# Decode attention in fp32: the vector engines' share of the value rows goes from 64 to 72 of 128, the row maxima are turned onto every partition, and two pieces of work change places

## The chip, the cores and the metric

The kernel runs on one core of a Trainium2 chip. The metric is device time in microseconds of one execution, as the median of several. The core has engines that run side by side, each through its own list of instructions in order: TensorE (PE, with its weight loads PEld), VectorE (DVE), ScalarE (ACT) and GpSimd (POOL). SyncE (SP) starts the large transfers from the chip's main memory (HBM), which 16 DMA engines carry out in the order in which SP issued them. Matrix products land in a small second memory, PSUM, here in tiles of 512 columns called `acc`, `bank` and `bank2`; GpSimd does not work on PSUM here.

## What is computed

One decode step of two transformer layers with shared weights and a shared cache: attention, a gated MLP, and both once more.

```python
q = (x @ wq).reshape(B, Sq, H, Dh)            # B = 2, Sq = 1, H = 32, Dh = 128
scores = einsum("bhqd,bhkd->bhqk", q, k_cache) * Dh ** -0.5     # Sk = 8192 keys a head
p = softmax(scores)
o = einsum("bhqk,bhkd->bhqd", p, v_cache)
x = x + o @ wo                                # then x = x + MLP(layernorm(x)); all of it twice
```

Everything is fp32. Keys and values of one layer are 2 x 268 MB, and each of the two layers reads nearly all of them, so that the core reads 1152.39 MB in one execution.

## The kernel before, in words

**Items.** A batch and two neighbouring heads form an item (the last two heads are items of their own, "singles"). Partition p holds `rows` = 128 keys of its head, 64 partitions for each of the two heads, so that the keys of an item are a tile of 128 partitions x 128 rows x 128 numbers, 64 KB a partition and 8192 KB in all; the values the same. One DMA brings the keys of an item, one its values. The arena (`space` in the traces) has room for three such tiles, and SP loads in the order K(n), V(n-1), K(n+1), V(n) and so on: each load takes the place of the third load ahead of it, and is issued once all readers of that one are done. Sixteen rows are a "part" (JC = 16), and a place is freed part by part. Layer 0 goes through the items upwards, layer 1 downwards.

**Scores.** The query of an item is spread over the partitions by a small matrix product (`query`, L687) into one of two stretches of `bank`. DVE multiplies the keys by it in three units of 48, 48 and 32 rows (`multiply`, L769). POOL adds the upper 64 numbers of each row to the lower 64 (L798). DVE sums what is left (`add_up`, L801), which is the score. The sum of the third unit of an item is made in the turn of the next item, ahead of its first product.

**Softmax.** `peak` takes the maximum of each partition's scores (L825) and turns the column of 128 maxima into a row, by a product of the column with the unit matrix (L827, into `turned`, a part of `bank2`). `highest` takes the maximum of each head from the row (L833, on one partition) and spreads it over the partitions by a second product (L835). `softmax` has ACT make the exponentials `prz` from it (L850, L858).

**Values.** TensorE multiplies the first 64 rows of each partition by their weights (`values`, L944, 16 products of four rows, each run in two passes). The other 64 rows (FOLD = 4 parts) are *folded* by DVE and POOL for all items but the first and last few of a layer (`folds`; 49 foldings in all). `weigh(n, True)` copies the weights of these rows into a stretch of `bank2` called `share` (L905) and has DVE multiply the first 32 rows by them (L912); POOL then adds halves onto each other, 32 rows to 16, to 8, to 4 (L915). `weigh(n, False)` does the same with the last 32 rows, one item later, and adds the two results of four rows (L917). `folded` adds the four rows into the accumulator by one product (L922), and frees the values' place.

**Order.** Each engine's order is the order in which `attention` writes it out, unit by unit; nothing reorders it. In the turn of item n, p is the item before it and f the one before p. Ahead of the first unit stand the last `add_up` and `peak` of p and `weigh(f, False)`. Behind the first unit (j == 0) stand the `query` of the next item and `folded(f)`; `highest` and `softmax` of p come at j == 0 too where p has three units. At j == 1 come the sums and `values(p)`, and every second item `gather` (L967, L968, DVE), which reads the finished accumulator; the items in between have a reciprocal there (`inverse`, L877). At j == 2 comes `weigh(p, True)`.

Accesses to the same PSUM tile by two engines are kept apart by waits: a product that writes `bank` or `bank2` holds up the DVE instruction behind it that uses the same tile.

Of the kernel before, what the change touches and what calls it, by code (L numbers as in the profile page):

```python
# [9 lines left out]
F32 = mybir.dt.float32  # L10
AF = mybir.ActivationFunctionType
ALU = mybir.AluOpType
AX = mybir.AxisListType
PSUM = bass.MemoryType.PSUM

P = 128
# [3 lines left out]
DH = 128  # L20
# [4 lines left out]
JC = 16  # L25
# [18 lines left out]
END = RING + NPLACE * PLACE  # L44
HELD = 5
SPLIT = (18, 18, 12, 16)
FOLD = 4


class Item:  # L50
# [75 lines left out]
def decode_layers(ctx, tc, x_in, kc, vc, wq, wo, wg, wu, wd, out):  # L126
# [32 lines left out]
    def part_at(at, n):  # L159
        return space[:, at:at + n]  # L160
# [180 lines left out]
    def name(kind, layer, n):  # L341

        return kind, 1 if n in (KEYS_HELD if kind == "k" else VALUES_HELD) else layer, n
# [170 lines left out]
    turned = bank2[:, 4 * GH:4 * GH + P]  # L514
    pair, four = bank2[:, 4 * GH + P:4 * GH + P + 2], bank2[:, 4 * GH + P + 2:4 * GH + P + 6]
    low = bank2[:, 4 * GH + P + 6:]
    share = low[:, :FOLD * JC]
    kept = psum1.tile([P, JC, DH], F32, name="kept")

    mid = bank[:, CW + 2 * DH:]  # L520
# [16 lines left out]
    def small(p, n):  # L537

        if n > 2:
            return turned[0:p, 0:n]  # L540
        return pair[0:p, 0:n]
# [70 lines left out]
    def attention(layer):  # L612
# [208 lines left out]
                ready.pop(key)  # L821

        def peak(n):
            m = work.tile([P, 1], F32, name="m")
            nc.vector.reduce_max(m, S[n][:, :ITEMS[n].rows], axis=AX.X)  # L825
            mT[n] = small(1, P)
            nc.tensor.transpose(mT[n], m, ident)  # L827

        def highest(n):

            heads = ITEMS[n].heads
            m1 = work.tile([1, 2], F32, name="m1")
            nc.vector.reduce_max(m1[:, :heads], mT.pop(n).rearrange("p (i q) -> p i q", i=heads), axis=AX.X)  # L833
            mT[n] = small(P, 2)
            nc.tensor.matmul(mT[n][:, :heads], ones[0:1, :], m1[:, :heads], start=True, stop=True)  # L835

        def weights_of(n):

            if ITEMS[n].heads == 2:
                return prz.rearrange("p a e -> p (a e)")  # L840
            return prz[:, n - PAIRS, :]
# [44 lines left out]
        def accumulator(n):  # L886
            return acc[:, (n // B + 1) % 2 if n < PAIRS else (n - PAIRS) // B, :]

        def completes(i):

            return i > 0 and ITEMS[seq[i - 1]].h == ITEMS[seq[i]].h

        def folds(n):

            return (2, 1)[layer] < n < PAIRS - 3

        def weigh(n, first):

            lo = ITEMS[n].parts - FOLD
            if first:  # L900
                of_halves = weights_of(n)[:, 8 + 4 * JC * lo:8 + 4 * JC * (lo + FOLD)]
                of_halves = of_halves.rearrange("p (g a e) -> p a g e", a=4, e=4)
                for i in range(2):
                    at = slice(i * HALF, i * HALF + HALF)
                    nc.scalar.copy(share[at].rearrange("p (g e) -> p g e", e=4), of_halves[at, i])  # L905
            rows = FOLD // 2 * JC
            begin = 0 if first else rows
            at = arena.live[name("v", layer, n), lo][0]
            t = part_at(at, FOLD * PART).rearrange("p (j d) -> p j d", d=DH)
            of_rows = share[:, begin:begin + rows].unsqueeze(2).to_broadcast([P, rows, DH])  # L910
            u = t[:, begin:begin + rows]
            nc.vector.tensor_tensor(out=u, in0=u, in1=of_rows, op=ALU.mult)  # L912
            while rows > 4:
                rows //= 2
                nc.gpsimd.tensor_tensor(out=u[:, :rows], in0=u[:, :rows], in1=u[:, rows:2 * rows], op=ALU.add)  # L915
            if not first:
                nc.gpsimd.tensor_tensor(out=t[:, :4], in0=t[:, :4], in1=u[:, :4], op=ALU.add)  # L917

        def folded(n):

            key, lo = name("v", layer, n), ITEMS[n].parts - FOLD
            nc.tensor.matmul(  # L922
                accumulator(n)[0:16, :], owner[:, 8 * ITEMS[n].b:8 * ITEMS[n].b + 16],
                part_at(arena.live[key, lo][0], 4 * DH), start=False, stop=completes(seq.index(n)),
            )
            for k in range(lo, lo + FOLD):
                done((key, k))
            ready.pop(key)

        def values(i, lo=0, hi=8):  # L930

            n = seq[i]
            it, key, pr = ITEMS[n], name("v", layer, n), weights_of(n)
            t = ready[key]
            left = not (layer == 0 and n in VALUES_HELD)
            gs, less = it.rows // 4, folds(n)
            if less:
                gs -= 4 * FOLD
            begins = not completes(i)
            for g in range(4 * lo, min(gs, 4 * hi)):  # L940
                c = g % 4
                m = 8 * it.heads
                at = m * g + m // 2 * (1 - it.b)
                nc.tensor.matmul(  # L944
                    accumulator(n)[32 * c:32 * c + m, :], pr[:, at:at + m],
                    t[g // 4][:, g % 4 * 4:g % 4 * 4 + 4, :].rearrange("p j d -> p (j d)"),
                    start=(begins and g < 4), stop=(completes(i) and g >= gs - 4 + less),
                )
                if left and g % 4 == 3:
                    done((key, g // 4))  # L950
            if left and 4 * hi >= gs and not less:
                ready.pop(key)
# [103 lines left out]
        for i, n in enumerate(seq):  # L1056
            last = i == N - 1
            p = seq[i - 1] if i else None

            v = {N - 2: None, N - 1: N - 3}.get(i, i - 1) if layer == 0 else i - 1  # L1060
            f = seq[i - 2] if i > 1 and folds(seq[i - 2]) else None
            a = seq[i - 2] if i > 1 and completes(i - 2) and not (layer == 0 and last) else None

            soon = layer == 1 and i in (1, 4)
            first = layer == 1 and i == 1
            us = units(n)

            ahead = p is not None and several(p)
            if first:
                query(seq[i + 1])  # L1070
            if first or ahead:
                add_up(p, *units(p)[-1])
                peak(p)
            if f is not None:
                weigh(f, False)
            if first:
                highest(p)
                softmax(p)
            for j, (k, m) in enumerate(us):
                multiply(n, k, m)  # L1080
                if j == 0 and not last and not first and (i or layer == 0):
                    query(seq[i + 1])
                if j == 0 and f is not None:
                    folded(f)
                if at_once(n, k) and k == 0:
                    add_up(n, k, m)
                if j == 1 and first:
                    values(v)
                    total(p)
                if j == 0 and p is not None and not first and not ahead:  # L1090
                    add_up(p, *units(p)[-1])
                    peak(p)
                if j == (0 if soon or ahead else 1) and p is not None and not first:
                    highest(p)
                    softmax(p)
                if j == (1 if several(n) else 2) and not first:
                    if p is not None:
                        total(p)
                        inverse(p)
                    if a is not None:  # L1100
                        gather(a)
                        if p < PAIRS:
                            context(a)
                    if v is not None and v >= 0:
                        values(v)
                    if a is not None and p >= PAIRS:
                        context(a)
                late_sum = len(us) == 3 and j > 0
                if late_sum and j == 2:
                    add_up(n, *us[0])  # L1110
                if j == 2 and i and folds(p):
                    weigh(p, True)
                if j > late_sum and (n, us[j - 1][0]) in prod:
                    add_up(n, *us[j - 1])
                if j == 3 and first:
                    inverse(p)
                if j == (2 if several(n) else 3) and a is not None and p < PAIRS:
                    divide(a, several(n))
                if j == 1 and late is not None:
                    divide(late)  # L1120
            late = a if a is not None and p >= PAIRS else None
            if layer == 1 and i == 0:

                nc.vector.scalar_tensor_tensor(qsb, acc[:, 0, :], rstd, qsb, op0=ALU.mult, op1=ALU.add)
# [3 lines left out]
        if layer == 0:  # L1128
            values(N - 2)
        peak(n)  # L1130
        highest(n)
        softmax(n)
        if layer == 0:
# [182 lines left out]
```

## Time and profile before

| | |
|---|---|
| median of three runs | 2679.16 us (2679.13 to 2679.84) |
| the profiled execution | 2680.14 us, of which the span from first to last instruction 2678.3 us |
| busy DVE, POOL, PE, ACT | 2194.3, 2015.2, 817.5, 186.2 us |
| read from HBM | 1152.39 MB, 430 GB/s over the span |

Times in the profile are from the start of the span. In rows of the timeline the first number is the start, the second the duration (of several instructions, from the first start to the last end), both in us; in brackets stands how long the engine had been idle before, and what ended that. In rows of groups, "x98 | 432.7, 4415 | 27.3" means 98 instructions, 432.7 us busy, 4415 ns each, 27.3 us of idle time ahead of them.

### The profile page before, as it was taken

The numbers are of one execution on the slowest core, as the hardware profiler recorded it, in microseconds if no ns is written. First come the engines' busy times: TensorE is split into PE (matmuls) and PEld (weight loads), VectorE is DVE, ScalarE is ACT, GpSimd is POOL, SyncE is SP. The second block draws the span as 40 slices with busy tenths as digits, with TensorE's granted clock in tenths as the row PEclk, the third lists the DMA queues.
The fourth block names the chain that finished last, engine by engine and source line by source line (L and its number), as shares of the span: only waits on it lengthen the run. The fifth ranks groups of instructions, "written<-read, shape, count | busy, mean of one in ns | idle before, by whom it ended". The sixth has DMA issues, their size and how long they took to land.

```text
span 2678.3 us, 13402 instructions
## 1 busy us (share of the span) xinstructions
PE 817.5 (31%) x5030; PEld 256.9 (10%) x5030; DVE 2194.3 (82%) x919; ACT 186.2 (7%) x890; POOL 2015.2 (75%) x608
## 2 busy tenths in 40 slices
PE   1312222232223222334663322222222222222266
PEld 0100000000000000011221000000000000000022
DVE  4869999999999999967038789999999999998940
ACT  0000000000000000001026000000000000000000
POOL 2548999998999989944028469899999988998930
PEclk8665555655555555566986655555565555655568
DMA  9999999999999999999999999999999999999999
GB/s 423 436 430 433 437 434 431 434 435 431 432 436 433 431 435 433 433 429 427 420 416 430 436 432 432 434 430 437 432 430 437 434 431 434 434 433 433 432 431 388
DMA packets 29336, 1153.26 MB, mean 431 GB/s; under 512 B 3384, under 2 KB 3416, under 8 KB 4184
## 3 DMA queue, kind: packets, MB, share of 16 engines
q1 hardware_dynamic: 29088, 1152.40, 99.8%
q8 instruction: 39, 0.64, 0.1%
q14 instruction: 25, 0.20, 0.0%
q10 hardware_dynamic: 184, 0.02, 0.0%
HBM read 1152.39 MB, written 0.01 MB: 430 GB/s over the span
## 4 chain that ended last, share of the span: by engine, by line
DMA 43%; DVE 38%; POOL 10%; PE 7%; issue 2%; ACT 1%; ACTq 0%; SPq 0%; POOLq 0%; DVEq 0%
DMA space<-in_A_k_cache_dram 33%; DVE space L769 19%; DVE scores L801 9%; DVE space L912 7%; POOL space L915 7%; DMA space<-in_A_v_cache_dram 4%; DMA space<-in_B_w_down_dram 2%; PE acc L944 2%; PE acc L922 2%; POOL space L798 1%; POOL space L917 1%; DMA space<-in_B_w_up_dram 1%; DMA space<-in_A_wo_dram 1%; PE bank L687 1%; PE acc L1026 1%
## 5 line engine op out<-in xcount | busy, mean ns | idle before, releaser
L798 POOL TENSOR_TENSOR space<-space 128x3072 f32<-128x3072 f32 (+4 forms) x221 | 1124.9, 5110 | 234.6 <-DVE space L769 196.1
L769 DVE TENSOR_TENSOR space<-space,bank 128x6144 f32<-128x6144 f32 (+4 forms) x223 | 1111.0, 4984 | 220.5 <-DMA space<-in_A_k_cache_dram 144.5
L915 POOL TENSOR_TENSOR space<-space 128x2048 f32<-128x2048 f32 (+2 forms) x294 | 796.9, 2710 | 163.5 <-DVE space L912 146.6
L801 DVE TENSOR_REDUCE scores<-space 128x48 f32<-128x3072 f32 (+4 forms) x223 | 563.9, 2550 | 17.5 <-POOL space L798 17.3
L944 PE MATMUL acc<-space,prz 128*16 128x512 f32 (+1 forms) x2528 | 430.0, 846 | 380.3 <-DMA space<-in_A_v_cache_dram 372.2
L912 DVE TENSOR_TENSOR space<-space,bank 128x4096 f32<-128x4096 f32 x98 | 432.7, 4415 | 27.3 <-PE bank L827 27.3
L827 PE MATMUL bank<-ident,m 128*1 128x128 f32 x68 | 24.4, 358 | 420.7 <-DVE m L825 420.6
L944 PEld LDWEIGHTS acc<-space,prz 128*16 128x16 f32 (+1 forms) x2528 | 87.1, 124 | 663.4 <-issue 464.4
L850 ACT ACTIVATE nbs<-bank 128x2 f32<-128x2 f32 (+1 forms) x68 | 11.6, 171 | 1937.9 <-PE bank L835 1904.5
L687 PE MATMUL bank<-qsb,home 36*128 36x128 f32 x60 | 23.4, 492 | 367.8 <-DVE space L769 351.1
L585 POOL TENSOR_TENSOR rstd<-ve,few 128x1 f32<-128x1 f32 x4 | 2.2, 561 | 174.4 <-DVE ve L583 174.4
L687 PE MATMUL bank<-qsb,wide 36*128 36x128 f32 x60 | 23.2, 486 | 348.3 <-DVE space L769 333.2
L922 PE MATMUL acc<-space,few 128*16 128x512 f32 x98 | 92.5, 1047 | 63.3 <-POOL space L917 63.3
L1227 DVE STREAM_TRANSPOSE gu<-acc 128x288 f32<-128x288 f32 x4 | 1.9, 482 | 85.5 <-ACT acc L1225 85.5
L917 POOL TENSOR_TENSOR space<-space 128x512 f32<-128x512 f32 x49 | 62.1, 1268 | 3.8
L858 ACT ACTIVATE prz<-scores,nbs 64x128 f32<-64x128 f32 (+1 forms) x128 | 50.7, 396 | 12.3 <-POOL prz L848 8.8
L827 PEld LDWEIGHTS bank<-ident,m 128*1 128x1 f32 x68 | 5.4, 79 | 477.6 <-issue 433.9
L687 PEld LDWEIGHTS bank<-qsb,home 36*128 36x128 f32 x60 | 14.7, 304 | 378.2 <-DVE space L769 360.3
L791 ACT ACTIVATE space<-space 128x128 f32<-128x128 f32 x164 | 48.4, 296 | 19.7 <-DVE space L769 16.6
L687 PEld LDWEIGHTS bank<-qsb,wide 36*128 36x128 f32 x60 | 14.5, 300 | 358.0 <-DVE space L769 341.6
L967 DVE TENSOR_TENSOR acc<-acc,few 128x512 f32<-128x512 f32 x34 | 23.5, 691 | 25.0 <-PE acc L944 25.0
L835 PE MATMUL bank<-m,few 1*128 1x2 f32 (+1 forms) x136 | 39.0, 354 | 15.1 <-DVE m L833 15.1
(120 smaller groups left out, 584.5 us busy)
## 6 DMA issues: line engine op xcount, KB each, us to landing
space<-in_A_v_cache_dram SPq DMA_DIRECT2D x7, 4096.0 KB
space<-in_A_k_cache_dram SPq DMA_DIRECT2D x6, 4096.0 KB
space<-in_B_w_gate_dram SPq DMA_DIRECT2D x9, 1152.0 KB
space<-in_B_w_up_dram SPq DMA_DIRECT2D x9, 1152.0 KB
space<-in_B_w_down_dram SPq DMA_DIRECT2D x8, 1152.0 KB
space<-in_A_wq_dram SPq DMA_DIRECT2D x9, 1024.0 KB
space<-in_A_wo_dram SPq DMA_DIRECT2D x2, 4608.0 KB
space<-in_A_k_cache_dram SPq DMA_DIRECT2D x4, 2048.0 KB
```

Source lines behind the costliest of these rows:

```text
L687: nc.tensor.matmul(qb[n], of_row, qsb[rows, m * DH:(m + 1) * DH], start=True, stop=True)
L769: nc.vector.tensor_tensor(out=u[:, :r, :], in0=t[:, :r, :], in1=qb[n].unsqueeze(1).to_broadcast([P, r, DH]), op=ALU.mult)
L791: nc.scalar.activation(u[:, j, :], u[:, j, :], AF.Copy, accum_out=S[n][:, base(n, k) + j:base(n, k) + j + 1])
L798: nc.gpsimd.tensor_tensor(out=half, in0=half, in1=u[:, :r, DH // 2:], op=ALU.add)
L801: nc.vector.tensor_reduce(out=S[n][:, base(n, k):base(n, k) + own_rows(n, k, m)], in_=prod.pop((n, k)), axis=AX.X, op=ALU.add)
L835: nc.tensor.matmul(mT[n][:, :heads], ones[0:1, :], m1[:, :heads], start=True, stop=True)
L858: nc.scalar.activation(pr[at, lo:].rearrange("p (g e) -> p g e", e=4)[:, 0:it.rows // 2 * it.heads:2 * it.heads, :], s[at, :it.rows].rearr ...
L912: nc.vector.tensor_tensor(out=u, in0=u, in1=of_rows, op=ALU.mult)
L915: nc.gpsimd.tensor_tensor(out=u[:, :rows], in0=u[:, :rows], in1=u[:, rows:2 * rows], op=ALU.add)
L917: nc.gpsimd.tensor_tensor(out=t[:, :4], in0=t[:, :4], in1=u[:, :4], op=ALU.add)
L922: nc.tensor.matmul(accumulator(n)[0:16, :], owner[:, 8 * ITEMS[n].b:8 * ITEMS[n].b + 16], part_at(arena.live[key, lo][0], 4 * DH), start=F ...
L944: nc.tensor.matmul(accumulator(n)[32 * c:32 * c + m, :], pr[:, at:at + m], t[g // 4][:, g % 4 * 4:g % 4 * 4 + 4, :].rearrange("p j d -> p ...
```

## The change

Five edits in one:

- FOLD counts rows now, and is 72: the first weighing takes 32 rows (EARLY), the second 40. POOL reduces 40 rows by adding the last 8 onto the first 8, and then as before from 32. TensorE multiplies 56 rows, in 14 products instead of 16.
- The column of maxima is given to TensorE 128 times over (`to_broadcast`), so that the product leaves the whole row of maxima on every partition of `turned`. `highest` takes the maxima of the two heads on all partitions and hands them to `softmax` from SBUF; the second product, L835, is gone.
- This product is a function of its own, `turn`, and is written behind `weigh(f, False)`; in `peak` it stood ahead of it.
- The query of the next item is written behind the third product of an item of three units; it stood behind the first.
- The fourth part of the values (rows 48 to 63) is read by both now, rows 48 to 55 by TensorE and the rest by the fold, and is freed by the fold.

```diff
-FOLD = 4
+FOLD = 72
+EARLY = 32
...
         def peak(n):
-            m = work.tile([P, 1], F32, name="m")
-            nc.vector.reduce_max(m, S[n][:, :ITEMS[n].rows], axis=AX.X)
-            mT[n] = small(1, P)
-            nc.tensor.transpose(mT[n], m, ident)
+            mT[n] = work.tile([P, 1], F32, name="m")
+            nc.vector.reduce_max(mT[n], S[n][:, :ITEMS[n].rows], axis=AX.X)
+
+        def turn(n):
+
+            m, mT[n] = mT[n], turned
+            nc.tensor.transpose(turned, m.to_broadcast([P, P]), ident)
 
         def highest(n):
 
             heads = ITEMS[n].heads
-            m1 = work.tile([1, 2], F32, name="m1")
-            nc.vector.reduce_max(m1[:, :heads], mT.pop(n).rearrange("p (i q) -> p i q", i=heads), axis=AX.X)
-            mT[n] = small(P, 2)
-            nc.tensor.matmul(mT[n][:, :heads], ones[0:1, :], m1[:, :heads], start=True, stop=True)
+            m1 = work.tile([P, 2], F32, name="m1")
+            nc.vector.reduce_max(m1[:, :heads], mT[n].rearrange("p (i q) -> p i q", i=heads), axis=AX.X)
+            mT[n] = m1
...
+        def folded_rows(n):
+
+            lo = ITEMS[n].rows - FOLD
+            at = arena.live[name("v", layer, n), lo // JC][0]
...
+            return lo, part_at(at + lo % JC * DH, FOLD * DH)
+
         def weigh(n, first):
...
-            rows = FOLD // 2 * JC
-            begin = 0 if first else rows
...
+            begin, end = (0, EARLY) if first else (EARLY, FOLD)
+            rows = end - begin
...
             nc.vector.tensor_tensor(out=u, in0=u, in1=of_rows, op=ALU.mult)
             while rows > 4:
-                rows //= 2
-                nc.gpsimd.tensor_tensor(out=u[:, :rows], in0=u[:, :rows], in1=u[:, rows:2 * rows], op=ALU.add)
+                less = 1 << (rows - 1).bit_length() - 1
+                nc.gpsimd.tensor_tensor(
+                    out=u[:, :rows - less], in0=u[:, :rows - less], in1=u[:, less:rows], op=ALU.add
+                )
+                rows = less
...
             if less:
-                gs -= 4 * FOLD
+                gs -= FOLD // 4
...
             if f is not None:
                 weigh(f, False)
+            if first or ahead:
+                turn(p)
...
-                if j == 0 and not last and not first and (i or layer == 0):
+                if j == (2 if len(us) == 3 else 0) and not last and not first and (i or layer == 0):
                     query(seq[i + 1])
```

Two engines' lists show what moves, each in the turn of one item in the middle of layer 0 (`bank_125` is `bank2`; "waits" names the engines or DMA queues whose semaphores an instruction waits for; lines of the changed kernel are 1 to 17 higher). TensorE, from the last value products of one item to the first of the next, before:

```order
L944 MATMUL acc<-space,prz 16x512 x15
L827 MATMUL bank_125<-ident,m 1x128 [waits DVE_49,Activation_49]
L687 MATMUL bank<-qsb,wide 128x128 [waits DVE_49]
L922 MATMUL acc<-space,few 16x512 [waits Pool_49]
L835 MATMUL bank_125<-m_763,few 128x2 [waits DVE_49]
L944 MATMUL acc<-space,prz 16x512 [waits DMAHW0_49,DVE_49,Activation_49]
```

and with the change:

```order
L957 MATMUL acc<-space,prz 16x512 x13
L688 MATMUL bank<-qsb,home 128x128 [waits DVE_49]
L831 MATMUL bank_125<-ident,m 128x128 [waits DVE_49,Activation_49]
L935 MATMUL acc<-space,few 16x512 [waits Pool_49]
L957 MATMUL acc<-space,prz 16x512 [waits DMAHW0_49,DVE_49,Activation_49]
```

The query has moved ahead of the turning of the maxima and stands right behind the value products; the product of the folded rows no longer has the spreading of the maxima behind it.

DVE in the same stretch, from the last sum of the item before to its third product, before:

```order
L801 TENSOR_REDUCE scores<-space 128x32 [waits Pool_49]
L825 TENSOR_REDUCE m<-scores 128x1 [waits DVE_49]
L912 TENSOR_TENSOR space<-space,bank_125 128x4096 [waits PE_49]
L769 TENSOR_TENSOR space<-space,bank 128x6144 [waits DMAHW1_49]
L833 TENSOR_REDUCE m_593<-bank_125 1x2
L769 TENSOR_TENSOR space<-space,bank 128x6144 [waits PE_49]
L877 RECIPROCAL rinv<-bank_125 128x4 [waits PE_49]
L769 TENSOR_TENSOR space<-space,bank 128x4096
```

and with the change:

```order
L802 TENSOR_REDUCE scores<-space 128x32 [waits Pool_49]
L826 TENSOR_REDUCE m<-scores 128x1 [waits DVE_49]
L921 TENSOR_TENSOR space<-space,bank_125 128x5120
L770 TENSOR_TENSOR space<-space,bank 128x6144 [waits DMAHW1_49,PE_49]
L837 TENSOR_REDUCE m_581<-bank_125 128x2 [waits PE_49]
L770 TENSOR_TENSOR space<-space,bank 128x6144
L880 RECIPROCAL rinv<-bank_125 128x4 [waits PE_49]
L770 TENSOR_TENSOR space<-space,bank 128x4096
```

The second weighing (40 rows, 5120 numbers) and the second product lose their waits for TensorE; the first product and the maxima of the heads have one instead. POOL's list gains one addition of 128x1024 in each second weighing, and SP issues the same transfers in the same order.

More of the change, by code (lines that the diff above doesn't have):

```diff
@@ L516, in decode_layers @@
     low = bank2[:, 4 * GH + P + 6:]
-    share = low[:, :FOLD * JC]
+    share = low[:, :FOLD]
     kept = psum1.tile([P, JC, DH], F32, name="kept")
@@ L895, in folds @@
             return (2, 1)[layer] < n < PAIRS - 3
+        def folded_rows(n):
+            lo = ITEMS[n].rows - FOLD
+            at = arena.live[name("v", layer, n), lo // JC][0]
+            assert all(arena.live[name("v", layer, n), k][0] == at + (k - lo // JC) * PART for k in range(lo // JC, 8))
+            return lo, part_at(at + lo % JC * DH, FOLD * DH)
         def weigh(n, first):
-            lo = ITEMS[n].parts - FOLD
+            lo, t = folded_rows(n)
             if first:
-                of_halves = weights_of(n)[:, 8 + 4 * JC * lo:8 + 4 * JC * (lo + FOLD)]
+                of_halves = weights_of(n)[:, 8 + 4 * lo:8 + 4 * (lo + FOLD)]
                 of_halves = of_halves.rearrange("p (g a e) -> p a g e", a=4, e=4)
@@ L905, in weigh @@
                     nc.scalar.copy(share[at].rearrange("p (g e) -> p g e", e=4), of_halves[at, i])
-            rows = FOLD // 2 * JC
-            begin = 0 if first else rows
[L908 to L911, printed above, removed]
+            begin, end = (0, EARLY) if first else (EARLY, FOLD)
+            rows = end - begin
+            t = t.rearrange("p (j d) -> p j d", d=DH)
+            u = t[:, begin:end]
+            of_rows = share[:, begin:end].unsqueeze(2).to_broadcast([P, rows, DH])
             nc.vector.tensor_tensor(out=u, in0=u, in1=of_rows, op=ALU.mult)
             while rows > 4:
-                rows //= 2
-                nc.gpsimd.tensor_tensor(out=u[:, :rows], in0=u[:, :rows], in1=u[:, rows:2 * rows], op=ALU.add)
+                less = 1 << (rows - 1).bit_length() - 1
[3 more added lines that the diff above has]
+                rows = less
             if not first:
@@ L919, in folded @@
         def folded(n):
-            key, lo = name("v", layer, n), ITEMS[n].parts - FOLD
+            key = name("v", layer, n)
+            lo, t = folded_rows(n)
             nc.tensor.matmul(
-                accumulator(n)[0:16, :], owner[:, 8 * ITEMS[n].b:8 * ITEMS[n].b + 16],
-                part_at(arena.live[key, lo][0], 4 * DH), start=False, stop=completes(seq.index(n)),
+                accumulator(n)[0:16, :], owner[:, 8 * ITEMS[n].b:8 * ITEMS[n].b + 16], t[:, :4 * DH],
+                start=False, stop=completes(seq.index(n)),
             )
-            for k in range(lo, lo + FOLD):
+            for k in range(lo // JC, ITEMS[n].parts):
                 done((key, k))
@@ L946, in values @@
                     t[g // 4][:, g % 4 * 4:g % 4 * 4 + 4, :].rearrange("p j d -> p (j d)"),
-                    start=(begins and g < 4), stop=(completes(i) and g >= gs - 4 + less),
+                    start=(begins and g < 4), stop=(completes(i) and g >= gs - 4 and not (less and c == 0)),
                 )
@@ L1092, in attention @@
                     peak(p)
+                    turn(p)
                 if j == (0 if soon or ahead else 1) and p is not None and not first:
@@ L1130, in attention @@
         peak(n)
+        turn(n)
         highest(n)
```

## The prediction

> **What bounds the kernel now.** I read the page first: busy times, the rows of the DMA and the chain that ended last.
>
> ```profile
> PE 817.5 (31%) x5030; PEld 256.9 (10%) x5030; DVE 2194.3 (82%) x919; ACT 186.2 (7%) x890; POOL 2015.2 (75%) x608
> DMA  9999999999999999999999999999999999999999
> GB/s 423 436 430 433 437 434 431 434 435 431 432 436 433 431 435 433 433 429 427 420 416 430 436 432 432 434 430 437 432 430 437 434 431 434 434 433 433 432 431 388
> q1 hardware_dynamic: 29088, 1152.40, 99.8%
> DMA 43%; DVE 38%; POOL 10%; PE 7%; issue 2%; ACT 1%; ACTq 0%; SPq 0%; POOLq 0%; DVEq 0%
> ```
>
> No slice of the span has the DMA engines below nine tenths, while DVE stands at 82%. The chain gives DVE 38% all the same, so I looked at whether the transfers ever wait for the engines. First the rate by stage: items without folding at the start of layer 0, then the folded items of layers 0 and 1.
>
> ```profile
> 45.00:200.00 155.00, 34.85 (x218) 11.89 (x218) 125.62 (x40) 5.04 (x22) 82.77 (x14) 0.60 1.00 433
> 240.00:1080.00 840.00, 211.12 (x915) 60.95 (x908) 782.26 (x251) 45.47 (x195) 764.86 (x219) 0.57 1.00 433
> 1640.00:2500.00 860.00, 218.39 (x929) 63.53 (x929) 801.17 (x259) 47.05 (x202) 783.21 (x223) 0.57 1.00 433
> ```
>
> Behind the stage come busy us of PE, PEld, DVE, ACT and POOL, the clock, the DMA share and GB/s. POOL is busy for 83 of 155 us in the first stage and for 765 of 840 in the second; the rate is 433 GB/s in each. The engines don't slow the transfers. Then two items from the timeline of layer 0, all engines together:
>
> ```profile
> 407.60 0.33 SPq L168 DMA_DIRECT2D space<-in_A_v_cache_dram  x1
> 408.45 4.42 DVE L912 TENSOR_TENSOR space<-space,bank 128x4096 f32<-128x4096 f32 x1 [0.56 <-PE bank L827]
> 412.95 8.29 POOL L915 TENSOR_TENSOR space<-space 128x2048 f32<-128x2048 f32 x3 [2.46 <-DVE space L912]
> 413.93 6.55 DVE L769 TENSOR_TENSOR space<-space,bank 128x6144 f32<-128x6144 f32 x1 [1.06 <-DMA space<-in_A_k_cache_dram]
> 421.37 6.55 DVE L769 TENSOR_TENSOR space<-space,bank 128x6144 f32<-128x6144 f32 x1 [0.69 <-PE bank L687]
> 422.55 17.87 POOL L798 TENSOR_TENSOR space<-space 128x3072 f32<-128x3072 f32 x3
> 422.64 1.89 PE L922 MATMUL acc<-space,few 128*16 128x512 f32 x2 [1.31 <-POOL space L917]
> 424.46 0.58 PE L835 MATMUL bank<-m,few 1*128 1x2 f32 x2
> 424.56 0.33 SPq L168 DMA_DIRECT2D space<-in_A_k_cache_dram  x1
> 426.35 0.59 PE L871 MATMUL bank<-few 128*128 128x4 f32 x2 [1.30 <-ACT prz L858]
> 427.84 0.17 DVE L877 RECIPROCAL rinv<-bank 128x4 f32<-128x4 f32 x1
> 427.93 4.39 DVE L769 TENSOR_TENSOR space<-space,bank 128x4096 f32<-128x4096 f32 x1
> 433.31 6.11 PE L944 MATMUL acc<-space,prz 128*16 128x512 f32 x32 [6.37 <-DMA space<-in_A_v_cache_dram]
> 435.50 4.41 DVE L912 TENSOR_TENSOR space<-space,bank 128x4096 f32<-128x4096 f32 x1
> 440.39 8.28 POOL L915 TENSOR_TENSOR space<-space 128x2048 f32<-128x2048 f32 x3
> 445.39 0.33 SPq L168 DMA_DIRECT2D space<-in_A_v_cache_dram  x1
> 445.40 0.29 DVE L825 TENSOR_REDUCE m<-scores 128x1 f32<-128x128 f32 x1
> 446.24 4.42 DVE L912 TENSOR_TENSOR space<-space,bank 128x4096 f32<-128x4096 f32 x1 [0.56 <-PE bank L827]
> 450.74 8.29 POOL L915 TENSOR_TENSOR space<-space 128x2048 f32<-128x2048 f32 x3 [2.07 <-DVE space L912]
> 452.63 6.55 DVE L769 TENSOR_TENSOR space<-space,bank 128x6144 f32<-128x6144 f32 x1 [1.96 <-DMA space<-in_A_k_cache_dram]
> 462.35 0.33 SPq L168 DMA_DIRECT2D space<-in_A_k_cache_dram  x1
> 466.54 0.69 DVE L967 TENSOR_TENSOR acc<-acc,few 128x512 f32<-128x512 f32 x1
> 467.87 4.41 DVE L769 TENSOR_TENSOR space<-space,bank 128x4096 f32<-128x4096 f32 x1
> 486.20 4.42 DVE L912 TENSOR_TENSOR space<-space,bank 128x4096 f32<-128x4096 f32 x1 [0.56 <-PE bank L827]
> 491.32 6.55 DVE L769 TENSOR_TENSOR space<-space,bank 128x6144 f32<-128x6144 f32 x1 [0.70 <-DMA space<-in_A_k_cache_dram]
> ```
>
> Each first product of an item waits for its keys, at 413.93, 452.63 and 491.32: 38.70 us an item, 19.35 us a transfer of 8.39 MB, which is 433.5 GB/s. SP issues each transfer while the one ahead of it still runs. Values are issued at 407.60, and the keys ahead of them are in use only at 413.93; keys are issued at 424.56, and the values ahead of them are in use at 433.31. So the values have a lead of 6.3 us (7.2 in the next item) and the keys one of 8.7. As long as these leads stay well above nothing, no engine costs time; the DVE share of the chain is the time from issue back to a release that came early enough.
>
> The page "DMA: Bandwidth & Descriptors" of the Trainium skill ("Where 436 GB/s comes from") gives the ports into the on-chip memory a ceiling of 435 GB/s; the 433.5 of these rows agrees. By it the transfers have at most 0.4% left (an estimate). The same section says that the main memory binds such loads at about 358 GB/s; that would make 1152.39 MB last 3219 us (an estimate), and the trace contradicts it with 430 GB/s over the span.
>
> **The change part by part.** The prices come from these groups and the rows above.
>
> ```profile
> L769 DVE TENSOR_TENSOR space<-space,bank 128x6144 f32<-128x6144 f32 x114 | 747.1, 6553 | 178.9 <-DMA space<-in_A_k_cache_dram 139.6 <-PE bank L687 39.2
> L912 DVE TENSOR_TENSOR space<-space,bank 128x4096 f32<-128x4096 f32 x98 | 432.7, 4415 | 27.3 <-PE bank L827 27.3
> L915 POOL TENSOR_TENSOR space<-space 128x1024 f32<-128x1024 f32 x98 | 230.4, 2351 | 7.7
> ```
>
> *The second weighing* has 5120 numbers in place of 4096. The trace has no such shape: its cost lies between 4.42 and 6.55 us (a product of 6144). The cost is linear between these two, (6.553 - 4.415) / 2048 = 1.044 ns a number, so I take 4.42 + 1.07 = 5.49; the ends keep +0 and +2.14 as bounds.
>
> *POOL's fourth addition* there is of 128x1024: 2.35 us, and 0.07 of gap, since three additions in a row take 8.28 where their parts sum to 0.15 less. That makes +2.42 us an item.
>
> *The waits of DVE.* The second weighing no longer stands behind the turning product: -0.56 an item. The second key product no longer stands behind the query: -0.70. What is late next: DVE reaches the next keys earlier and waits for them, as it does now for 139.6 us in all.
>
> *The query* goes behind the value products on TensorE. It can start when those are through, at 433.31 + 6.11 = 439.4, and its taker, the first product of the next item, waits for keys until 452.63: 13 us of cover. Two products fewer an item only widen it.
>
> *The turned maxima.* The product with 128 columns of weights resembles L871 (128 columns, 0.59 for two passes); before it took 0.37. I take 0.6, with 0.3 and 1.2 as bounds. It now waits for the second weighing and has the whole first product, 6.5 us, until DVE asks for the row. Queued behind it is the product of the folded rows, which waits for POOL some 10 us longer anyway. The spreading product (0.58) goes, and with it its wait behind the folded rows, so that the softmax comes about 4 us earlier (L835 ran at 424.46, four us after the first product's end at 420.48). Its takers wait for the values' transfer in any case (L944 at 433.31): nothing.
>
> *Engines by item.* DVE: from 408.45 to 446.24 there are 37.79 us, of which 0.56, 1.06 and 0.69 are waits, so 35.5 of work; with the gather, from 446.24 to 486.20, it is 39.96 - 1.96 - 0.70 - 0.56 = 36.7. With +1.07 that is 36.6 and 37.8, below 38.70. POOL: from 412.95 to 450.74 there are 37.79 - 2.07 = 35.7; with +2.42 it is 38.1. It still fits, with 0.6 us to spare.
>
> *The ring.* DVE and POOL also wait for each other, and this is the narrowest place. From the third product (427.93) to the maximum (445.40) DVE needs 17.47. Then come 0.25 for the maximum, 5.49 for the second weighing, and what lies between its end and the next issue of keys, 462.35 - 446.24 - 4.42 = 11.69, and 2.42 more for POOL's addition: 37.3 us to the end of the folded product. From there DVE's next third product follows behind L871 and the reciprocal (0.59 + 0.17, 38.1 in all) or behind the gather (467.87 - 466.54 = 1.33 and the handing over, 38.7). The mean is 38.4, against 38.70 for two transfers. So the ring fits too, by 0.3 us an item. Before, the weighing and POOL's adding made it 2.9 us shorter (1.07 + 2.42 - 0.56), and it never closed.
>
> *Transfers.* Values are issued behind the last score sum, whose place in the turn hardly moves: lead 6 us. Keys are issued behind the folded product, later by 1.07 + 2.42 - 0.56 = 2.9 us: lead 8.7 - 2.9 = 5.8. No transfer starts later.
>
> *The ends.* After layer 1's last folded item the POOL work of the last item starts 2.9 us later, and about 0.7 comes back from the dropped product. Weights are already queued there:
>
> ```profile
> 2602.79 6.15 SPq L257 DMA_DIRECT2D space<-in_B_w_up_dram  x2
> 2642.10 11.80 PE L1216 MATMUL acc<-space,xt 128*8 128x288 f32 x144 [10.33 <-DMA space<-in_B_w_up_dram]
> ```
>
> The `w_up` load would be issued 2 us later and is used 39 us after its issue, when PE has waited 10.33 us for it: nothing.
>
> The sum is 0 + 0 + 0 on the profiled execution's 2680.14 us. That one stands 1.0 us above the median of the runs, so I predict the median again: 2679.2 us. A measurement of this kernel can tell 0.2%, or 5.4 us, from no change.
>
> **The rivals.**
>
> *A: the ring becomes longer than two transfers.* For it speaks that the ring takes 38.4 of 38.70 now. It begins to matter at 0.3 us an item above my prices, eats up the lead of 5.8 us over the 24 or 25 folded items of a layer (another 0.24 an item), and so delays transfers from +0.54 an item on. The one price without a row of its own is the second weighing. At its upper bound (+1.07 above what I took) the loss is (1.07 - 0.54) x 49 = 26 us, 2705 us; at half of that excess there is none. Against it speaks that the three products with shapes of their own (6553, 4415, and 4.39 in the key product of 4096) lie on one line.
>
> *B: the engines' order sets the pace, and removed waits are gained.* Then 27.3 us (L912) and 39.2 us (L769) come back, less 49 x 1.07 = 52 us of longer weighing: 2665 us. The chain's 38% for DVE speaks for it; against it speak the 139.6 us for which DVE waits for keys, and the even 433 GB/s.
>
> *C: the waits only move.* The first product waits for the query now. If the value products were late, by the 13 us of cover, each item would lose what lies beyond. Nothing in the rows comes near it, and the time would be 2679 us again.
>
> **How the numbers follow.** The forecast of no change gets 0.86, A 0.09, B 0.03, C 0.02. A part of A stays below 5.4 us (0.01), so slower by over 0.2% has 0.08, within 0.2% has 0.89, and faster has 0.03. The forecast's own spread is that of single runs, 2679.1 to 2680.1, and a few tenths for transfers that land unevenly; the lower end takes 2 us for an unforeseen gain at the ends, the upper end the beginning of A, where a layer loses 2 us: 2677 to 2683.5.
>
> **What would show it.** In the profile of the changed kernel the second weighing should last 5.5 us without a wait for PE, POOL's four additions 10.7, and the second key product should follow the maxima at once. First products should still wait for keys, 38.70 us apart, with POOL busy for some 2130 us in all. Keys should be issued 5 to 6 us ahead of the landing of the values. The prediction is wrong if the DMA share falls below one in the folded stages, or if first products stop waiting for keys and follow DVE's earlier work at once.

## The result, and the profile after

The changed kernel takes 2694.29 us (median of 6 runs, 2692.62 to 2694.95) against 2679.22 for the one before in the same session: a ratio of 1.0052, with a 95% interval from 1.0042 to 1.0062. It is slower by 15 us, where no change was forecast. The span of the profiled execution grew from 2678.3 to 2692.3 us, by 14.0. The page, in the order of the lines shown of before:

```profile
PE 766.0 (28%) x4698; PEld 219.3 (8%) x4698; DVE 2257.9 (84%) x919; ACT 189.0 (7%) x890; POOL 2128.2 (79%) x657
DMA  9999999999999999999999999999999999999998
GB/s 421 437 435 435 431 431 434 432 436 392 425 435 434 433 433 435 431 430 426 419 422 436 432 434 433 432 434 432 434 385 435 435 432 431 432 435 434 433 428 382
q1 hardware_dynamic: 29088, 1152.40, 99.4%
DMA 37%; DVE 33%; POOL 16%; PE 7%; issue 6%; ACT 1%; SPq 0%; ACTq 0%; POOLq 0%; DVEq 0%
```

The row of GB/s gives the answer's place at once. Two slices stand out: the tenth with 392 and the thirtieth with 385, one in each layer; a general lack of room would have lowered all the slices of the folded items. The windows confirm it (columns as before; the last two are the DMA share and GB/s). First the two folded stages, then 16 us about each of the two places, all of the changed kernel:

```profile
240.00:1080.00 840.00, 193.76 (x786) 48.18 (x778) 804.48 (x250) 46.43 (x195) 808.38 (x237) 0.57 0.99 429
1640.00:2500.00 860.00, 199.21 (x800) 49.65 (x796) 824.07 (x256) 45.97 (x194) 827.46 (x243) 0.57 1.00 430
640.00:656.00 16.00, 0.45 (x1) 0.18 (x1) 15.97 (x6) 0.00 (x0) 9.59 (x4) 0.50 0.71 287
1958.00:1974.00 16.00, 0.45 (x1) 0.18 (x1) 15.97 (x6) 0.00 (x0) 9.66 (x4) 0.50 0.67 270
```

Measured against the 433.5 GB/s of steady transfers, the first window lacks (433.5 - 287) / 433.5 x 16 = 5.4 us and the second 6.0: 11.4 of the 14.0 us. (The rest is found further down.) What DVE and POOL do there, from the timeline of layer 0:

```profile
617.80 17.83 POOL L799 TENSOR_TENSOR space<-space 128x3072 f32<-128x3072 f32 x3
621.79 4.41 DVE L770 TENSOR_TENSOR space<-space,bank 128x4096 f32<-128x4096 f32 x1
626.12 5.13 DVE L669 COPY wide<-few 128x128 f32<-128x128 f32 x1
631.17 4.54 DVE L669 COPY home<-few 128x128 f32<-128x128 f32 x1
635.63 3.34 DVE L802 TENSOR_REDUCE scores<-space 128x48 f32<-128x3072 f32 x1
638.89 4.40 DVE L921 TENSOR_TENSOR space<-space,bank 128x4096 f32<-128x4096 f32 x1
643.37 8.29 POOL L924 TENSOR_TENSOR space<-space 128x2048 f32<-128x2048 f32 x3 [7.75 <-DVE space L921]
648.78 0.33 SPq L169 DMA_DIRECT2D space<-in_A_v_cache_dram  x1
654.38 6.54 DVE L770 TENSOR_TENSOR space<-space,bank 128x6144 f32<-128x6144 f32 x1
```

and the same two copies in the kernel before, with the POOL instruction beside them and the issue of the same load:

```profile
613.91 0.22 DVE L668 COPY wide<-few 128x128 f32<-128x128 f32 x1
613.92 1.33 POOL L917 TENSOR_TENSOR space<-space 128x512 f32<-128x512 f32 x1
614.05 1.29 DVE L668 COPY home<-few 128x128 f32<-128x128 f32 x1
640.73 0.33 SPq L168 DMA_DIRECT2D space<-in_A_v_cache_dram  x1
```

Behind `query` stand two DVE copies (`pairs_of`), which refill the tiles `wide` and `home` with the pattern that spreads a query. They run only at the start of a layer, ahead of the folded items, and when the head number passes 16, once a layer in the middle of the folded items. The change moved them with the query, from behind the first product to behind the third, and there they last 5.13 and 4.54 us (5.06 and 4.54 in layer 1) where they had taken 0.22 and 1.29. The load of values, which waits for DVE's score sums, was issued at 648.78 instead of 640.73, and the first product at 654.38 waits for nothing. In the two short windows above the DMA engines run dry: their shares are 0.71 and 0.67.

The copies' ends show why they are long. POOL's three sums run from 617.80 to 635.63; at 6.70 us each for the first two, the second ends at 631.2 and the third at 635.6. The first copy ends at 631.25 and the second at 635.71: each ends as the POOL instruction in progress ends. The profile has it as busy time of the copy, not as a wait.

### The profile page after: what moved, and what is told of

It reads as the page before. It is cut to its first block, busy times and chain, and to the rows that moved or that the text cites. A ratio compares the mean times of both kernels' runs of the same rounds, so it can differ in the third digit from the quotient of the medians.

```text
span 2692.3 us, 12933 instructions
## 1 busy us (share of the span) xinstructions
PE 766.0 (28%) x4698; PEld 219.3 (8%) x4698; DVE 2257.9 (84%) x919; ACT 189.0 (7%) x890; POOL 2128.2 (79%) x657
## 4 chain that ended last, share of the span: by engine, by line
DMA 37%; DVE 33%; POOL 16%; PE 7%; issue 6%; ACT 1%; SPq 0%; ACTq 0%; POOLq 0%; DVEq 0%
DMA space<-in_A_k_cache_dram 22%; DVE space L770 15%; POOL space L924 12%; DVE space L921 9%; DMA space<-in_A_v_cache_dram 8%; DVE scores L802 7%; PE acc L957 3%; DMA space<-in_B_w_down_dram 2%; POOL space L799 2%; PE acc L935 2%; POOL space L929 1%; DMA space<-in_A_wo_dram 1%; DMA space<-in_B_w_up_dram 1%; DMA space<-in_A_wq_dram 1%; DVE home L981 1%
## 5 line engine op out<-in xcount | busy, mean ns | idle before, releaser
L924 POOL TENSOR_TENSOR space<-space 128x1024 f32<-128x1024 f32 (+2 forms) x343 | 912.3, 2663 | 72.6 <-DVE space L921 51.9
L921 DVE TENSOR_TENSOR space<-space,bank 128x4096 f32<-128x4096 f32 x98 | 484.4, 4943 | 0.0
L831 PE MATMUL bank<-ident,m 128*128 128x128 f32 x68 | 29.8, 439 | 661.5 <-DVE space L921 614.6
L853 ACT ACTIVATE nbs<-m 128x2 f32<-128x2 f32 (+1 forms) x68 | 13.8, 203 | 1805.9 <-DVE m L837 1805.9
L831 PEld LDWEIGHTS bank<-ident,m 128*128 128x128 f32 x68 | 11.9, 175 | 675.7 <-issue 481.0
L935 PEld LDWEIGHTS acc<-space,few 128*16 128x16 f32 x98 | 6.3, 107 | 587.0 <-POOL space L929 587.0
L786 POOL TENSOR_TENSOR space<-space,qs 128x512 f32<-128x512 f32 x23 | 29.2, 1273 | 16.6 <-ACT qs L767 16.2
L994 PE MATMUL bank<-few,home 128*64 128x4 f32 (+2 forms) x136 | 17.5, 252 | 77.2 <-DVE home L981 77.2
L915 ACT COPY bank<-prz 64x72 f32<-64x72 f32 x98 | 21.3, 217 | 247.3 <-DVE rinv L880 149.6
```

What stands on the lines that cost most here:

```text
L786: nc.gpsimd.tensor_tensor(out=u[:, rows:every, :], in0=t[:, rows:every, :], in1=q.unsqueeze(1).to_broadcast([P, every - rows, DH]), op=ALU ...
L831: nc.tensor.transpose(turned, m.to_broadcast([P, P]), ident)
L924: nc.gpsimd.tensor_tensor(out=u[:, :rows - less], in0=u[:, :rows - less], in1=u[:, less:rows], op=ALU.add)
L935: nc.tensor.matmul(accumulator(n)[0:16, :], owner[:, 8 * ITEMS[n].b:8 * ITEMS[n].b + 16], t[:, :4 * DH], start=False, stop=completes(seq.i ...
```

## The experiments

Theory 1: these copies are the whole loss; the larger fold fits. Theory 2, rival A of the prediction: the ring of DVE and POOL spends the lead of the transfers item by item, and the copies only stand where it ran out.

**The copies behind the first product** (the query stays behind the third):

```diff
                 multiply(n, k, m)
+                if j == 0 and len(us) == 3 and not last and not first and ITEMS[seq[i + 1]].heads == 2:
+                    pairs_of(ITEMS[seq[i + 1]].h // 16)
```

> The changed kernel, with the two copies that refill the tiles `wide` and `home` for a query (once a layer, when the heads pass 16) written behind the first product again; the query itself stays behind the third. Theory 1 (the moved copies): the copies lasted 5.1 and 4.5 us beside POOL's sums and ran a transfer late, and nothing else costs time; the time is that of the kernel before, 2679 us (2678 to 2681). Theory 2 (the ring of DVE and POOL, longer by the larger fold, uses up the lead item by item, and the copies only mark the place where it ran out): the time stays near 2694 us, at least above 2688.

Measured: 2679.2 us, ratio to the kernel before 0.9995 (0.9986 to 1.0004). The folded stages are back at the old rate, with all of the larger fold in them:

```profile
240.00:1080.00 840.00, 196.54 (x786) 48.70 (x778) 803.93 (x252) 47.07 (x198) 815.87 (x239) 0.57 1.00 433
1640.00:2500.00 860.00, 200.46 (x797) 50.14 (x797) 822.33 (x258) 48.05 (x202) 832.93 (x246) 0.57 1.00 433
```

Theory 2 falls: the only thing undone is the place of the copies, and of the eight in the whole program only the four that run in the middle of the layers were long. At the old place the first copy of a pair still lasts 1.44 us in layer 0, to the end of a POOL addition, and this costs nothing.

**The query alone**, moved in the kernel before:

```diff
-                if j == 0 and not last and not first and (i or layer == 0):
+                if j == (2 if len(us) == 3 else 0) and not last and not first and (i or layer == 0):
                     query(seq[i + 1])
```

> The kernel before, with one edit: the query of the next item stands behind the third product, the copies with it. Theory 1: the copies last 4 us each there, until POOL's sums end, and shift DVE by some 6.5 us where the lead of the values' load is 5.3 us in layer 0 and 3.5 in layer 1; each layer loses 4 to 6 us, so 2687 to 2691 us. Theory 2: with the old fold the ring has 2.9 us more room an item, the time stays 2679 us.

Measured: 2684.35 us (ten runs, 2684.14 to 2685.76), ratio 1.0015 (1.0005 to 1.0024). The direction is theory 1's; the size is about half of what I expected. The timeline says why:

```profile
614.20 17.86 POOL L798 TENSOR_TENSOR space<-space 128x3072 f32<-128x3072 f32 x3
626.05 1.59 DVE L668 COPY wide<-few 128x128 f32<-128x128 f32 x1
627.56 4.58 DVE L668 COPY home<-few 128x128 f32<-128x128 f32 x1
645.21 0.33 SPq L168 DMA_DIRECT2D space<-in_A_v_cache_dram  x1
```

With the small fold POOL's sums begin at 614.20 instead of 617.80, while DVE reaches the copies at the same time. The first copy finds the second sum nearly done (614.20 + 2 x 6.7 = 627.6) and lasts 1.59 us instead of 5.13. The load is issued 3.6 us earlier than in the changed kernel. So the larger fold seems to have a part in the 15 us after all: the 3.6 us by which POOL's sums begin later agree with the 1.07 + 2.42 us that it adds ahead of them, and there they hold the copies longer. (The two kernels differ in the turned maxima as well, and no run has the query's move with the fold alone.)

**The query back**, in the changed kernel (the inverse of the diff above):

> The changed kernel, with the query and its copies behind the first product as before; the larger fold, the turned maxima and the order of the second weighing stay. Theory 1: 2679 us (2678 to 2682), as the wait of 0.7 us for the query comes back on DVE but fits into the item's 38.7 us. Theory 2: 2694 us or more, since DVE even has 0.7 us less room an item.

Measured: 2680.76 us, ratio 1.000 (0.999 to 1.0009): theory 1. The DVE wait for the query is back (39.0 us in all on the key products) and costs nothing that can be measured.

**The copies on ScalarE:**

```diff
-                nc.vector.tensor_copy(
+                nc.scalar.copy(
                     to.rearrange("p (i q) -> p i q", i=2), both[:, s * B + b, :].unsqueeze(2).to_broadcast([P, 2, HALF])
```

> The changed kernel, with the two copies made by ScalarE at the place they have in it, behind the third product. Theory 1, in the form that DVE's copy waits for the POOL instruction in progress: ScalarE's copies take a few tenths of a us each and hold up nobody; 2679 us (2678 to 2681). If what matters is the place (the copies wait for the tiles to be free there, whichever engine makes them), ScalarE's copies are long too, but DVE goes on, so the query is late, not DVE: the copies' durations tell this apart. Theory 2: 2694 us.

Measured: 2680.6 us, ratio 1.000 (0.9991 to 1.001). In layer 0 ScalarE makes them in 0.30 and 0.29 us. Nothing holds them up until DVE's third product, so they run at 615.5, ahead of POOL's sums, but still beside POOL's work:

```profile
608.35 8.31 POOL L924 TENSOR_TENSOR space<-space 128x2048 f32<-128x2048 f32 x3
615.53 0.30 ACT L669 COPY wide<-few 128x128 f32<-128x128 f32 x1
615.74 0.29 ACT L669 COPY home<-few 128x128 f32<-128x128 f32 x1
```

POOL's additions run until 616.66; the copies are done at 615.83 and 616.03. So DVE is relieved, and ScalarE's copies did not wait for this POOL work; beside the sums they were not tried.

**The copies as sums over one number**, on DVE and at the place of the change:

```diff
-                nc.vector.tensor_copy(
-                    to.rearrange("p (i q) -> p i q", i=2), both[:, s * B + b, :].unsqueeze(2).to_broadcast([P, 2, HALF])
+                nc.vector.reduce_sum(
+                    to.rearrange("p (i q) -> p i q", i=2),
+                    both[:, s * B + b, :].unsqueeze(2).to_broadcast([P, 2, HALF]).unsqueeze(3), axis=AX.X,
                 )
```

> The changed kernel, with the two refilling copies left on DVE and behind the third product, but made by another operation: a sum over one number, the form of the score sums, which the traces show beside POOL's work at their usual time. Theory 1a (DVE's fp32 copy, of all its operations, waits for the POOL instruction in progress): the two sums take 0.2 to 0.3 us each and the time is that of the kernel before, 2679 to 2681 us. Theory 1b (any DVE instruction that refills these tiles there waits, by the tiles or the place): they take 4 to 5 us each and the time stays at 2694.

Measured: 2679.17 us, ratio 0.9996 (0.9986 to 1.0006). From the timeline, right behind the third product:

```profile
626.19 0.28 DVE L669 TENSOR_REDUCE wide<-few 128x128 f32<-128x128 f32 x1
626.38 0.28 DVE L669 TENSOR_REDUCE home<-few 128x128 f32<-128x128 f32 x1
```

The same data at the same place in 0.28 us. So neither the tiles nor the place is at fault: it is the form of the instruction.

**Small copies everywhere**, added to the first of these kernels:

```diff
+                if j == 2 and len(us) == 3:
+                    nc.vector.tensor_copy(work.tile([P, 2], F32, name="tiny"), both[:, 0, :])
```

> The changed kernel with the copies behind the first product, and in addition one small DVE copy (128x2) behind the third product of every item of three units, whose result nobody uses. Theory 1a: however small, it lasts until the POOL instruction in progress ends, 1 to 6 us, instead of the 0.1 to 0.2 us of such a small operation; each item then has several us too much, and the time is far above 2679, 2780 to 2980 us. Rival: the wait depends on the size or on the tiles that are refilled; the small copies take under 0.3 us and the time stays at 2679 to 2681 us.

Measured: 2933.69 us, ratio 1.0945 (1.0922 to 1.0969). The group of these copies:

```profile
L1101 DVE COPY tiny<-few 128x2 f32<-128x2 f32 x57 | 309.5, 5431 | 0.0
```

and one of them with POOL's sums, from the timeline:

```profile
630.78 17.81 POOL L799 TENSOR_TENSOR space<-space 128x3072 f32<-128x3072 f32 x3
637.74 6.41 DVE L1101 COPY tiny<-few 128x2 f32<-128x2 f32 x1
```

Two numbers a partition take 5.4 us on average. The copy shown ends at 644.15, where the second sum ends (630.78 + 2 x 6.69 = 644.16). All 57 start while one POOL instruction is in progress, and each ends 0.02 to 0.03 us after that one. The copy's size does not set its time; POOL does.

**The fold alone**, without the other edits, and **a fold of 76 rows**, to see whether the ring was counted rightly. The first takes `peak` and `highest` from the kernel before and has the query behind the first product; the second is the first experiment with one number changed:

```diff
-FOLD = 72
+FOLD = 76
```

> The kernel before with the fold of 72 rows (steps of 32 and 40) and none of the other edits: the maxima are turned as before and ahead of the second weighing, spread by the second product, and the query stands behind the first product. If the ring as I counted it holds, it is longer here than in the changed kernel by 0.56 us (the weighing's wait for the turning) and, every second item, by 1.8 us (the reciprocal behind spreading and softmax), 39.9 us against 38.70: a loss of 1.2 x 49 = 57 us less about 5 us of lead a layer, near 2726 us (2705 to 2745). If the ring has more room than counted, 2679 us.

> The changed kernel with the copies behind the first product, and 76 rows folded in steps of 32 and 44. Against 72 rows the weighing gets 512 numbers more (0.53 us) and POOL's first addition has 1536 in place of 1024 (about 1.1 us). If the ring as I counted it holds (38.4 us at 72 rows), it has 40.0 here, 1.3 us above two transfers: 1.3 x 49 = 64 us less some 10 of lead, near 2733 us (2710 to 2755). If the ring has 1.6 us more room than counted, 2679 us.

Measured: 2733.09 us (ratio 1.0196, 1.018 to 1.0212) for the fold alone, and 2735.12 us (1.0203, 1.0187 to 1.0219) for 76 rows. In layer 0's folded stage of the one and of the other:

```profile
240.00:1080.00 840.00, 210.16 (x817) 60.26 (x813) 781.18 (x244) 45.76 (x195) 793.16 (x232) 0.57 0.99 421
240.00:1080.00 840.00, 195.12 (x733) 47.35 (x729) 790.69 (x244) 46.55 (x195) 814.80 (x232) 0.56 0.99 420
```

Here the rate is low over the whole stage, without any engine's busy share reaching one: this is what rival A looks like. The forecasts from the ring were 2726 and 2733 us. The ring was counted to within about 0.2 us an item. The fold alone differs from the run with the query back (2680.76 us) in the turning of the maxima only: the 72 rows fit only because the turning stands behind the weighing and the spreading product is gone. Which of the two is needed was not tried.

## Why the prediction was wrong, point by point

- *What bounds the kernel*: right. The transfers set the time, and in the four kernels that keep the rest of the change and take the late copies off DVE (copies early, query back, on ScalarE, as sums) the folded stages run at 432 or 433 GB/s.
- *The second weighing, POOL's fourth addition*: right. The products of 5120 numbers take 5477 ns (5.49 forecast), the four additions 10.75 us together (654.54 in layer 0; 10.7 forecast), and the second weighings wait for nothing any more:

```profile
L770 DVE TENSOR_TENSOR space<-space,bank 128x6144 f32<-128x6144 f32 x114 | 746.4, 6548 | 134.6 <-DMA space<-in_A_k_cache_dram 134.6
L921 DVE TENSOR_TENSOR space<-space,bank 128x5120 f32<-128x5120 f32 x49 | 268.4, 5477 | 0.0
L924 POOL TENSOR_TENSOR space<-space 128x1024 f32<-128x1024 f32 x147 | 345.8, 2352 | 44.0 <-DVE space L921 36.4
```

- *The waits of DVE, the turned maxima*: right. Key products of 6144 numbers wait for keys alone.
- *The query*: this is the step that failed. I priced it as a product on TensorE, with 13 us of cover, and left out what else it issues: in the middle of each layer, two DVE copies. So they went into the sum at nothing; measured, they hold DVE for 9.7 us a layer and have no cover at all. In the list of before they stood as two short rows (0.22 and 1.29 us), and the 1.29 was the sign: it ended at 615.34, with a POOL instruction (613.92 + 1.33 = 615.25) too. That the first took 0.22 was luck: it started at 613.91, just ahead of that instruction.
- *The ring*: the margin of 0.3 us an item was right, but I used it against steady costs alone. A single delay of 9.7 us in it meets a lead of about 6 us, whoever causes it. Behind the late load the first products follow DVE and no longer wait for their keys, so the ring can be read there by itself. Three of them in a row, in layer 1:

```profile
2010.31 6.54 DVE L770 TENSOR_TENSOR space<-space,bank 128x6144 f32<-128x6144 f32 x1
2049.05 6.55 DVE L770 TENSOR_TENSOR space<-space,bank 128x6144 f32<-128x6144 f32 x1
2087.08 6.55 DVE L770 TENSOR_TENSOR space<-space,bank 128x6144 f32<-128x6144 f32 x1
```

  They are 38.74 us apart (the item with the gather) and 38.03 (the one with the reciprocal); counted were 38.7 and 38.1. So the lead is rebuilt slowly, by about 0.3 us an item. Both signs of being wrong that the prediction names are there: first products without a wait for keys, and a DMA share of 0.99 in layer 0's folded stage.
- *Transfers*: the steady leads came out no shorter than forecast (keys issued at 619.82, the values ahead of them in use at 626.72: 6.9 us against 5.8); the load behind the copies, one in each layer, had none.
- *Rival A* had the right sign and the right place (the ring) but the wrong cause; its price of 26 us was for a weighing that costs more than it does.

The remaining 2.6 us (14.0 - 11.4) lie behind the windows, which end before the late load has landed. The value products that wait for their load show when values land, in the changed kernel:

```profile
626.72 4.99 PE L957 MATMUL acc<-space,prz 128*16 128x512 f32 x28 [6.93 <-DMA space<-in_A_v_cache_dram]
672.13 6.16 PE L957 MATMUL acc<-space,prz 128*16 128x512 f32 x28 [3.04 <-DMA space<-in_A_v_cache_dram]
1944.69 6.47 PE L957 MATMUL acc<-space,prz 128*16 128x512 f32 x28 [6.97 <-DMA space<-in_A_v_cache_dram]
2028.81 5.38 PE L957 MATMUL acc<-space,prz 128*16 128x512 f32 x28 [1.58 <-DMA space<-in_A_v_cache_dram]
```

In layer 0 one item takes 45.41 us instead of 38.70, and in layer 1 two items take 84.12 instead of 77.40: 6.7 us lost in each, 13.4 of the 14.0. Only part of this is the late issue. The keys ahead of the load were due at 607.32 + 38.70 = 646.0 (the first product at 607.32 waited for its keys), so it was issued 2.8 us late at 648.78. It then took 23.35 us to its use, 4.0 more than the 19.35 of a load that follows another without a gap. Why was not tried.

## What to carry to other kernels

When a step is moved, list everything that its function issues, also what it issues only now and then; a rare instruction on a loop with little room costs time once its delay exceeds the lead of the transfers, and here more than the excess: a load issued 2.8 us late came 6.7 us late. A row whose time differs between two instances of one shape (0.22 and 1.29 us here) can hold a wait that the profile books as work: look at what the neighbour engine was doing when it ended. And an engine at 84% can already be part of a closed ring: add up the chain around it, not its busy time.

## What the hardware showed

A DVE copy of fp32 from SBUF to SBUF does not run beside a POOL operation in progress here: it lasts until that ends, 5.13 and 4.54 us in the changed kernel and 5.4 on average for two numbers a partition, against 0.22 without one. DVE's sums, and its products with one operand in PSUM, run beside the same POOL work at their usual time: 0.28 us for the copies as sums, 4.41 for the key product of 4096 numbers at 621.79, beside POOL's sums, against 4.40 for the weighing of as many at 638.89, while POOL is idle. The page "SBUF — State Buffer" of the Trainium skill ("Terms", the shared port pair) says that DVE and GpSimd share a pair of ports under an exclusive lock that is held for a whole instruction, and that the loser blocks; these runs agree for DVE's copies, and add that a waiting copy is done when the POOL operation in progress ends, though the next one follows without a gap (the copy at 626.12 ends at 631.25, and POOL's three sums last 17.83 us, against 17.87 at 422.55 in the kernel before, where no copy ran beside them).
